# Attention in a stage of its own, and the first FFN products by Strassen's seven products on pairs of batches

## The chip, the cores and the metric

One NeuronCore of a Trainium2 chip runs the whole program. The metric is the device time of one execution in microseconds, the median of three runs for the kernel before. TensorE (PE) multiplies, VectorE (DVE), ScalarE (ACT) and GpSimd (POOL) do the work on tiles, and SyncE (SP) issues most transfers between DRAM and the on-chip memory.

## What is computed

Sigmoid attention for 8 batches, 12 heads, 448 positions and a head width of 64, then a bilinear feed-forward part on the 3584 tokens. All inputs are float32.

```python
scores = scale * np.matmul(q, k.transpose(0, 1, 3, 2)) - np.log(S)
attn = 1.0 / (1.0 + np.exp(-scores))
x = (attn @ v).transpose(0, 2, 1, 3).reshape(B * S, H * D)   # 3584 x 768
a = x @ w1                                                    # 768 x 1024
b = x @ w2
h = a * b @ w3                                                # 1024 x 1024
return h @ w_out                                              # 1024 x 768
```

## The kernel before, in words

Products are made in two ways. A float32 matmul is issued as it is, and shows as two matmul records. An fp32r matmul is one record; to keep precision each operand is split into a rounded part and a rest (`split`, lines 72 to 74), and a product is three fp32r matmuls: high by high, high by low, low by high.

Heads go in 48 pairs (two heads of 64 fill 128 rows). The first 13 pairs (`PLAIN`) use float32: a chunk of 128 positions takes two score matmuls (line 201), one on rows 0 to 63 and one on rows 64 to 127 of the array, and two sums with v (line 253), one on each half of the array's columns. Between the score and the sum stands one sigmoid on ACT (line 184). The weights w1 and w2, which come as 64-bit words, are decoded meanwhile by ACT (line 83) and DVE (lines 90 to 106), and split into fp32r parts that stay on chip.

The other 35 pairs use fp32r on the full array (lines 204, 230 and 260). They take 28 matmuls of 448 columns for a pair, two sigmoids for a chunk (one rounded, one full) and a subtraction on DVE (line 222). Into their matmuls the first products `up` (line 377) are mixed, 12 matmuls at a time: x times w1 and x times w2, on tiles of 512 tokens, 18 matmuls for each of 7 x 8 x 2 results, 2016 in all. The result g = a * b goes to `g_dram`.

After attention the last seventh of the first products runs alone, while w_out is decoded. Then w3 times w_out is made once (line 662, 384 matmuls of 384 columns). The last product, g times that matrix, is made by Strassen's seven products on pairs of batches (`products`, line 695, 1008 matmuls of 448 columns in four blocks); its operands are sums of blocks of g, made on DVE and ACT by `plain_operands`, `sum_operands` and `late_operands` from tiles `graw` that are loaded from `g_dram` into four buffers. Their names are a11, a12, s2, s3, a22, s1, s4 in the order of use.

The order on PE and SP is that of the code (`manual_schedule`), on ACT and POOL too in the attention's first part; the other engines' order is set by a scheduler when the program is built.

## Time and profile before

| | before |
|---|---|
| median of three runs | 1054.52 us (1053.53 to 1056.56) |
| profiled execution, its own time | 1054.23 us |
| its span, first to last instruction | 1052.4 us |
| PE busy | 1040.3 us, 99% |
| DVE busy | 796.3 us, 76% |
| ACT busy | 593.6 us, 56% |
| POOL busy | 163.1 us, 15% |
| moved by DMA | 164.41 MB, 156 GB/s over the span |
| granted TensorE clock, mean | 1.000 of full speed |

The busy time of an engine is the time in which at least one of its instructions runs. Matmuls overlap, so the mean length of one is longer than the distance from one to the next; that distance is read from the start times or from a stretch divided by its count. A wait of an engine is shown with what ended it.

### The profile page before, as it was taken

The page shows a single profiled execution, that of the slowest core. Times are in us where ns is not written, and L with a number is a line of the kernel's source. Part 1 is how long each engine was busy: PE and PEld are TensorE (multiplying, and loading weights), DVE is VectorE, ACT ScalarE, POOL GpSimd, SP SyncE. Part 2 cuts the span into 40 slices and gives each one's busy share as a digit, 9 for nine tenths or more (in the row PEclk, how much of TensorE's full clock was granted, in tenths as well). Part 3 has the DMA queues.
Part 4 walks back from the last instruction along what each step waited for, and adds up shares of the span by engine and source line. Part 5 has one row for each costly group of instructions (what it writes and reads, how often), then busy time and mean ns, then how long its engine had stood idle before and what let it go on. Part 6 is the DMA issues. An engine that isn't in the chain of part 4 may idle for free.

```text
span 1052.4 us, 14185 instructions
## 1 busy us (share of the span) xinstructions
PE 1040.3 (99%) x4820; PEld 847.4 (81%) x4820; DVE 796.3 (76%) x1254; ACT 593.6 (56%) x877; POOL 163.1 (15%) x249
## 2 busy tenths in 40 slices
PE   9999999999999999999999999999999999999998
PEld 3222788888888888888888888878899999999997
DVE  6998788877887778887878877668826677768672
ACT  6887766666666766676676666652324443323230
POOL 0000423323131322323232332100000000000000
PEclk9999999999999999999999999999999999999999
DMA  8676474564546554464455635144324555656542
GB/s 271 218 229 213 129 198 112 150 168 124 151 130 169 147 146 127 135 168 134 133 149 149 169 112 149 48 159 126 116 93 144 184 185 194 218 179 216 182 148 79
DMA packets 117255, 164.41 MB, mean 156 GB/s; under 512 B 9984, under 2 KB 95168, under 8 KB 117184
## 3 DMA queue, kind: packets, MB, share of 16 engines
q1 hardware_dynamic: 117184, 163.52, 51.9%
q8 instruction: 38, 0.62, 0.3%
q14 instruction: 33, 0.27, 0.1%
HBM read 124.16 MB, written 39.32 MB: 155 GB/s over the span
## 4 chain that ended last, share of the span: by engine, by line
PE 89%; DVE 5%; DMA 3%; ACT 1%; issue 1%; SPq 0%; ACTq 0%; DVEq 0%
PE up L377 41%; PE up L695 20%; PE av L260 9%; PE sp L204 8%; PE up L662 5%; PE av L253 2%; PE sp L201 2%; PE sp L230 1%; DMA graw<-g_dram 1%; DVE f L98 1%; DVE raw L103 1%; DMA raw<-w 1%; DMA raw<-w_out 1%; DVE w L74 1%; PE up L427 1%
## 5 line engine op out<-in xcount | busy, mean ns | idle before, releaser
L377 PE MATMUL up<-xh,w 128*128 128x512 f32 x1344 | 438.9, 391 | 1.4 <-DVE g L391 1.4
L377 PEld LDWEIGHTS up<-xh,w 128*128 128x128 f32 x1344 | 252.4, 188 | 54.8 <-ACT f L83 1.8
L377 PE MATMUL up<-xl,w 128*128 128x512 f32 x672 | 263.1, 392 | 0.0
L184 ACT ACTIVATE ah<-sp,bias 128x896 fp32r<-128x896 f32 x105 | 106.1, 1011 | 124.5 <-PE sp L204 124.5
L222 DVE TENSOR_TENSOR al<-sp,ah 128x896 fp32r<-128x896 f32 x105 | 114.4, 1090 | 63.2 <-ACT sp L184 62.4
L377 PEld LDWEIGHTS up<-xl,w 128*128 128x128 f32 x672 | 126.2, 188 | 23.3
L74 POOL TENSOR_TENSOR kl<-kk,kh 128x896 fp32r<-128x896 f32 x35 | 74.7, 2134 | 395.7 <-DVE kh L73 255.4
L695 PE MATMUL up<-gs,w 128*128 128x448 f32 x576 | 119.3, 367 | 0.0
L695 PEld LDWEIGHTS up<-gs,w 128*128 128x128 f32 x576 | 108.1, 188 | 9.9
L184 ACT ACTIVATE sp<-sp,bias 128x896 f32<-128x896 f32 x105 | 102.0, 972 | 0.0
L260 PE MATMUL av<-ah,vs 128*128 128x448 f32 x280 | 92.0, 369 | 0.4 <-DVE t L192 0.4
L695 PE MATMUL up<-ga,w 128*128 128x448 f32 x432 | 89.5, 366 | 0.0
L695 PEld LDWEIGHTS up<-ga,w 128*128 128x128 f32 x432 | 81.1, 188 | 7.1
L204 PE MATMUL sp<-qs,kh 128*128 128x448 f32 x210 | 77.4, 369 | 0.0
L260 PE MATMUL av<-al,vs 128*128 128x448 f32 x210 | 77.4, 368 | 0.0
L204 PE MATMUL sp<-qs,kl 128*128 128x448 f32 x210 | 77.2, 368 | 0.0
L74 POOL TENSOR_TENSOR vs<-vv,vs 128x256 fp32r<-128x256 f32 x70 | 54.9, 786 | 109.2 <-DVE vs L73 109.2
L73 ACT CAST ga<-graw 128x448 fp32r<-128x448 f32 x48 | 25.7, 566 | 68.6 <-DMA graw<-g_dram 68.6
L244 DVE TENSOR_TENSOR ah<-st,ah 64x448 fp32r<-64x448 f32 x70 | 44.2, 632 | 25.2 <-ACT st L184 23.7
L184 ACT ACTIVATE ah<-st,bias 64x448 fp32r<-64x448 f32 x70 | 46.9, 669 | 24.9 <-DVE st L192 23.6
L260 PEld LDWEIGHTS av<-ah,vs 128*128 128x128 f32 x280 | 52.6, 188 | 9.2 <-issue 1.2
L184 ACT ACTIVATE ap<-sp,bias 128x896 f32<-128x896 f32 (+1 forms) x52 | 52.1, 1004 | 13.4 <-PE sp L201 12.5
(77 smaller groups left out, 1504.1 us busy)
## 6 DMA issues: line engine op xcount, KB each, us to landing
graw<-g_dram SPq DMA_DIRECT2D x72, 448.0 KB, 4.4
qq<-qT SPq DMA_DIRECT2D x70, 224.0 KB, 3.7
kk<-kT SPq DMA_DIRECT2D x70, 224.0 KB, 4.4
g_dram<-g SPq DMA_DIRECT2D x56, 256.0 KB, 2.2
raw<-w SPq DMA_DIRECT2D x15, 768.0 KB, 5.4
vv<-vL SPq DMA_DIRECT2D x48, 192.0 KB, 3.8
xr<-x_dram SPq DMA_DIRECT2D x36, 256.0 KB, 4.4
raw<-w3T SPq DMA_DIRECT2D x16, 512.0 KB, 4.3
```

The source lines that it names most:

```text
L73: hi_engine(out=dst_hi, in_=src)
L74: lo_engine.tensor_tensor(out=dst_lo, in0=src, in1=dst_hi, op=ALU.subtract)
L184: nc.scalar.activation(dst, src, AF.Sigmoid, bias=bias[:n], scale=scale)
L201: nc.tensor.matmul(sp[:, j], kh[rows, at:at + n], qs[rows], start=True, stop=True)
L204: nc.tensor.matmul(sp[:, j], k[:, j, at:at + n], qs[:, j], start=m == 0, stop=m == 1)
L222: nc.vector.tensor_tensor(out=al, in0=sp, in1=ah, op=ALU.subtract)
L244: nc.vector.tensor_tensor(out=a[others, j], in0=t[rows], in1=a[rows, j], op=ALU.subtract)
L253: nc.tensor.matmul(accs[0][cols, :S], v[:ops[0].shape[0], c, cols], ops[0][:, j], start=first, stop=last,)
L260: nc.tensor.matmul(accs[j][:, :S], v[:, c, j].rearrange("p u d -> p (u d)"), a[:, j], start=first and m == 0, stop=last and m == len(ops) - 1,
L377: nc.tensor.matmul(acc[:, :TU], w[fc // NH][:, fc % NH, kc], x, start=(kc == 0 and m == 0), stop=(kc == NK - 1 and m == 2),)
L662: nc.tensor.matmul(acc[:, :NM], a[:, jc], w[:, jc, ms], start=(jc == 0 and m == 0), stop=(jc == NF - 1 and m == 2),)
L695: nc.tensor.matmul(acc[:, :TB], w[:, c, ms], g[:, c], start=(c, m) == (0, 0), stop=(c, m) == (NH - 1, 2),)
```

## The change

Attention becomes a stage of its own with nothing mixed in. One pair stays float32. For the other 47, q and k are split on DVE (`qh`, `ql`), and a chunk's scores are six fp32r matmuls, three for each head, with the two heads on rows 0 to 63 and 64 to 127. There is one sigmoid for a chunk, kept in float32, and the sums with v are float32 matmuls on column halves, all eight of a pair in one piece after the next pair's scores. The decoding of w1 and w2 is spread over 44 pairs; DVE also makes four differences of weight blocks (`piece_sum`), which go to `t_dram`.

After attention all first products are made by Strassen's scheme: the two rows of blocks are two batches of x (448 tokens each), the inner dimension is cut in halves of 384, and the columns are w1 and w2. For each of 4 x 8 units there are seven products of nine matmuls of 448 columns, 2016 in all. The block sums of x are made by `operand_x`, the results are put together on DVE by `unit_step`, multiplied on POOL and stored by POOL's own DMA queue. w_out and w3 are decoded meanwhile and stored in DRAM in the same way. The product w3 times w_out keeps its matmuls. The last product keeps its seven products; its operand s2 is now made in the last stage and no longer ahead of it.

```diff
-    PLAIN = 2 * NPAIR + 1
...
+    PLAIN = 1
...
+    def split_pair(p, qk):
+        if p < PLAIN:
+            return (qk,)
+        hi = pa.tile([P, 2, S], F32R, name="qh")
+        lo = pa.tile([P, 2, S], F32R, name="ql")
+        split(hi, lo, qk, nc.vector.tensor_copy, nc.vector)
+        return hi, lo
+
...
+    def scores(qks, c):
         at, n = CHUNKS[c]
-        sp = ps.tile([P, 2, 512], F32, name="sp", bufs=2)[:n, :, :S]
-        for j in range(2):
-            if kl is None:
+        sp = ps.tile([P, 2, 512], F32, name="sp", bufs=3)[:n, :, :S]
+        terms = ((0, 0), (0, 1), (1, 0)) if len(qks) > 1 else ((0, 0),)
+        for m, (kt, qt) in enumerate(terms):
+            for j in range(2):
                 rows = slice(j * D, (j + 1) * D)
-                nc.tensor.matmul(sp[:, j], kh[rows, at:at + n], qs[rows], start=True, stop=True)
-                continue
-            for m, k in enumerate((kh, kl)):
-                nc.tensor.matmul(sp[:, j], k[:, j, at:at + n], qs[:, j], start=m == 0, stop=m == 1)
+                nc.tensor.matmul(
+                    sp[:, j], qks[kt][rows, 1, at:at + n], qks[qt][rows, 0],
+                    start=m == 0, stop=m == len(terms) - 1,
...
+    def attention(sp):
         n = sp.shape[0]
-        if plain:
-            a = pa.tile([P, 2, S], F32, name="ap", tag="ah", bufs=3)[:n]
-            sigmoid(a, sp)
-            return (a,)
-        ah = pa.tile([P, 2, S], F32R, name="ah", tag="ah", bufs=3)
-        sigmoid(ah[:n], sp)
-        sigmoid(sp, sp)
-        if n < P:
-
...
-    def attend(c, ops, v, accs):
-
-        first, last = c == 0, c == NC - 2
...
+    def attend(v, aps):
+        acc = ps.tile([P, 512], F32, name="av", bufs=2)
+        for c, a in enumerate(aps):
             for j in range(2):
                 cols = slice(j * D, (j + 1) * D)
                 nc.tensor.matmul(
-                    accs[0][cols, :S], v[:ops[0].shape[0], c, cols], ops[0][:, j],
-                    start=first, stop=last,
+                    acc[cols, :S], v[:a.shape[0], c, cols], a[:, j], start=c == 0, stop=c == NC - 1
                 )
-            return
-        for j in range(2):
-            for m, a in enumerate(ops):
-                nc.tensor.matmul(
-                    accs[j][:, :S], v[:, c, j].rearrange("p u d -> p (u d)"), a[:, j],
...
+    def piece_sum(fc, kind):
+        f1, f2 = fs[2 * fc], fs[2 * fc + 1]
+        b11, b21, b12, b22 = f1[:, :KH], f1[:, KH:], f2[:, :KH], f2[:, KH:]
+        a, b = {
+            0: lambda: (b12, b11), 3: lambda: (b22, sums[0]), 2: lambda: (b22, b12), 1: lambda: (b21, sums[3])
+        }[kind]()
+        t = sums[kind] = pd.tile([P, KH, P], F32, name="ts", bufs=4)
+        nc.vector.tensor_tensor(out=t, in0=a, in1=b, op=ALU.subtract)
+        hl = pd.tile([P, 2, KH, P], F32R, name="th", bufs=4)
+        split(hl[:, 0], hl[:, 1], t, nc.vector.tensor_copy, nc.vector)
+        store_later(t_dram[fc, kind], hl.bitcast(F32))
+
+    steps = []
+    for i in range(2 * NF):
+        at = 2 + 13 * i // 5
+        steps += [(at - 2, piece_load, (i,)), (at - 1, piece_magnitude, (i,)), (at, piece_decode, (i,))]
+        steps += [(at + 1, piece_split, (i,))]
+        if i % 2:
+            steps += [(at + 1, piece_sum, (i // 2, 0)), (at + 2, piece_sum, (i // 2, 3))]
+            steps += [(at + 2, piece_sum, (i // 2, 2)), (at + 3, piece_sum, (i // 2, 1))]
+    DONE = max(at for at, _, _ in steps) + 1
...
+    def operand_x(name, x1, x2):
+        top, bottom = slice(0, KH), slice(KH, NK)
+        src = {
+            "a11": x1[:, top], "a12": x1[:, bottom], "s3": x2[:, top], "s2": x2[:, top],
+            "a22": x2[:, bottom], "s1": x1[:, top], "s4": x1[:, bottom],
+        }[name]
+        work = {
+            "s3": (x1[:, top], x2[:, top], ALU.subtract),
+            "s2": (x2[:, bottom], x2[:, top], ALU.subtract),
+            "s1": (x2[:, top], x1[:, top], ALU.add),
+            "s4": (x1[:, bottom], x2[:, top], ALU.subtract),
+        }.get(name)
+        if work is not None:
+            nc.vector.tensor_tensor(out=src, in0=work[0], in1=work[1], op=work[2])
+        split(*xop[name], src, nc.scalar.copy, nc.vector)
...
+        now, aps = aps, []
+        if p < len(pairs):
+            qk = parts.pop(p)
+            for c in range(NC):
+                aps.append(attention(scores(qk, c)))
+        if p + 1 < len(pairs):
+            parts[p + 1] = split_pair(p + 1, qks.pop(p + 1))
+        for at, f, args in steps:
+            if at == p and f is not piece_load:
+                f(*args)
+        if DONE <= p < DONE + EARLY:
+            operand_x(names[p - DONE], *xs)
+        if p > 0:
+            b, kc = pairs[p - 1]
+            store_later(x_dram[kc, :, b * S:(b + 1) * S], attend(vvs.pop(p - 1), now))
...
+    def load_sums(fcs, name):
+        for fc in fcs:
+            t = pt.tile([P, 2, KH, P], F32R, name="tw")
+            nc.sync.dma_start(out=t.bitcast(F32), in_=t_dram[fc, KINDS[name]])
+            sets[fc, name] = (t[:, 0], t[:, 1])
...
+    def x_product(fc, name):
+        acc = ps2.tile([P, 512], F32, name="up", tag="acc", bufs=8)
+        ws = weights(fc, name)
+        for c in range(KH):
+            for m, (w, x) in enumerate(((0, 0), (0, 1), (1, 0))):
+                nc.tensor.matmul(
+                    acc[:, :S], ws[w][:, c], xop[name][x][:, c],
+                    start=(c, m) == (0, 0), stop=(c, m) == (KH - 1, 2),
+                )
+        return acc[:, :S]
...
+    def unit_step(g, fc, name):
+        acc = x_product(fc, name)
+        if name == "a11":
+            us[fc] = pu.tile([P, S], F32, name="u")
+            nc.scalar.copy(out=us[fc], in_=acc)
+            return
+        u = us[fc]
+        if name == "a12":
+            rs[fc] = pu.tile([P, 2, S], F32, name="r", bufs=3)
+            add(rs[fc][:, 0], acc, u)
+        elif name == "s3":
+            p7s[fc] = acc
+        elif name == "s2":
+            add(u, acc, u)
+            vs[fc] = pu.tile([P, S], F32, name="v")
+            add(vs[fc], p7s.pop(fc), u)
+        elif name == "a22":
+            add(rs[fc][:, 1], acc, vs[fc])
+        elif name == "s1":
+            add(vs[fc], acc, vs[fc])
+            add(u, acc, u)
+            r = rs[fc]
+            nc.gpsimd.tensor_tensor(out=r[:, 1], in0=r[:, 1], in1=vs.pop(fc), op=ALU.mult)
+        else:
+            add(u, acc, u)
+            r = rs.pop(fc)
+            nc.gpsimd.tensor_tensor(out=r[:, 0], in0=r[:, 0], in1=us.pop(fc), op=ALU.mult)
+            at = 2 * g * S
+            nc.gpsimd.dma_start(
+                out=g_dram[fc, :, at:at + 2 * S].rearrange("p (t s) -> p t s", t=2), in_=r
+            )
...
+            f = decode(raw, magnitude(raw, pu, 2))
+            if i + 2 < len(todo):
+                nxt.append(load_words(todo[i + 2][0], pu, 2))
+            nc.gpsimd.dma_start(out=dst, in_=f)
...
+        for i, name in enumerate(names):
+            for fc in fcs:
+                unit_step(g, fc, name)
+            if nxt is not None and i and names[i - 1] in KINDS:
+                load_sums(nxt[1], names[i - 1])
+            if i in (1, 4) and k:
+                take(decodes, 1)
+            if turn:
+                operand_x(name, *xs)
+            if nxt is None and i < 4:
+                load_out(*list(wo_tags)[2 + i])
+            if nxt is None and i in (4, 5):
+                w3_chunk(i - 4)
+        if k % NH == 1 and g + 1 < NG:
+            xs = load_xs(g + 1)
...
-    early = itertools.chain(plain_operands(0), sum_operands(0, ("s2",)))
+    early = plain_operands(0)
...
-        stage = spare[:, c % 2]
+        w3 = w3s.pop(i)
+        if not second:
+            stage = px2.tile([P, 4, NM], F32, name="stage", tag="s4", bufs=1)
...
+    for name in ("s2", "s1", "s4", "s3", "a22"):
+        operand(p5, name)
+    total = p5.tile([P, NH, TB], F32, name="total", bufs=1)
...
-    prepare_ = itertools.chain(sum_operands(0, ("s3", "a22")), late_operands(0))
+    prepare_ = itertools.chain(
+        sum_operands(0, ("s2",)), sum_operands(0, ("s3", "a22")), late_operands(0)
+    )
```

On PE, in the attention of before, a piece of the order from the fp32r pairs: `sp` are scores, `up` the first products, each row an instruction or several of the same form.

```order
L204 MATMUL sp<-qs,kh 128x448
L204 MATMUL sp<-qs,kl 128x448
L204 MATMUL sp<-qs,kh 128x448
L204 MATMUL sp<-qs,kl 128x448
L377 MATMUL up<-xh,w 128x512
L377 MATMUL up<-xl,w 128x512
L377 MATMUL up<-xh,w 128x512 x2
L377 MATMUL up<-xl,w 128x512
L377 MATMUL up<-xh,w 128x512 x2
L377 MATMUL up<-xl,w 128x512
L377 MATMUL up<-xh,w 128x512 x2
L377 MATMUL up<-xl,w 128x512
```

The same place after the change, one pair p from its second row on: 22 of its 24 score matmuls (`qh`, `ql` are the parts of q and k), then the sums of pair p - 1.

```order
L166 MATMUL sp<-ql,qh 128x448 x2
L166 MATMUL sp<-qh,ql 128x448 x2
L166 MATMUL sp<-qh 128x448 x2
L166 MATMUL sp<-ql,qh 128x448 x2
L166 MATMUL sp<-qh,ql 128x448 x2
L166 MATMUL sp<-qh 128x448 x2
L166 MATMUL sp<-ql,qh 128x448 x2
L166 MATMUL sp<-qh,ql 128x448 x2
L166 MATMUL sp<-qh 64x448 x2
L166 MATMUL sp<-ql,qh 64x448 x2
L166 MATMUL sp<-qh,ql 64x448 x2
L183 MATMUL av<-ap,vv 64x448 x8
```

What moved: the `up` rows have left the attention, the scores went from four full-array matmuls to six half-array ones for a chunk, and the sums with v stand in one piece.

On DVE, before, near the end of the stage of w3 times w_out: `spare<-graw` is the sum that s3 and s1 start from (`total` in the code), `w` are parts of the weight sums.

```order
L574 TENSOR_TENSOR spare<-graw 128x448
L574 TENSOR_TENSOR graw<-graw 128x448
L574 TENSOR_TENSOR spare<-spare 128x384
L574 TENSOR_TENSOR spare<-graw 128x448
L74 TENSOR_TENSOR w<-spare,w 128x384
L574 TENSOR_TENSOR graw<-graw 128x448
L74 TENSOR_TENSOR w<-spare,w 128x384
L574 TENSOR_TENSOR spare<-spare 128x384 x2
L74 TENSOR_TENSOR w<-spare,w 128x384 x3
L574 TENSOR_TENSOR spare<-spare 128x384
```

After the change this is what DVE does at the start of the last stage: `gs_7222` is s2, `o` and `u` take results of the last product from PE.

```order
L74 TENSOR_TENSOR gs_7222<-graw,gs_7222 128x448 x3
L512 TENSOR_TENSOR graw<-graw 128x448
L512 TENSOR_TENSOR o<-up,u 128x448
L512 TENSOR_TENSOR graw<-graw 128x448
L74 TENSOR_TENSOR gs_7222<-graw,gs_7222 128x448
L512 TENSOR_TENSOR o<-up,u 128x448 x2
L512 TENSOR_TENSOR u<-up,u 128x448
L512 TENSOR_TENSOR total<-graw 128x448
L74 TENSOR_TENSOR ga_7226<-graw,ga_7226 128x448
L512 TENSOR_TENSOR graw<-graw 128x448
```

What moved: the first two `total` rows stood inside the stage of w3 times w_out, ahead of its last weight sums; now the first one stands in the last stage, behind the four splits of s2 and a result of the third of the seven products.

## Rows read from the trace of the kernel before

**Rows 1.** The page: busy us by engine (share of the span), instructions.

```profile
PE 1040.3 (99%) x4820; PEld 847.4 (81%) x4820; DVE 796.3 (76%) x1254; ACT 593.6 (56%) x877; POOL 163.1 (15%) x249
```

**Rows 2.** The chain that ended last, shares by engine and line.

```profile
PE up L377 41%; PE up L695 20%; PE av L260 9%; PE sp L204 8%; PE up L662 5%; PE av L253 2%; PE sp L201 2%; PE sp L230 1%; DMA graw<-g_dram 1%; DVE f L98 1%; DVE raw L103 1%; DMA raw<-w 1%; DMA raw<-w_out 1%; DVE w L74 1%; PE up L427 1%
```

**Rows 3.** Windows: stretch, busy us (instructions) by engine, clock, DMA share, GB/s.

```profile
7.60:107.20 99.60, 95.28 (x413) 24.35 (x412) 92.17 (x134) 81.52 (x102) 2.60 (x4) 1.00 0.75 234
107.20:708.90 601.70, 599.89 (x2714) 508.20 (x2712) 471.89 (x685) 400.97 (x565) 160.27 (x242) 1.00 0.50 141
709.00:774.50 65.50, 65.50 (x289) 54.24 (x290) 45.88 (x102) 17.22 (x34) 0.00 (x0) 1.00 0.35 105
774.40:842.50 68.10, 66.99 (x385) 66.34 (x384) 40.10 (x68) 30.00 (x57) 0.00 (x0) 1.00 0.46 159
842.50:1052.40 209.90, 206.48 (x1010) 189.12 (x1008) 145.13 (x263) 61.88 (x117) 0.00 (x0) 1.00 0.54 176
```

**Rows 4.** Timeline of PE, fp32r attention: start, length, line, tiles.

```profile
302.31 0.37 PE L204 MATMUL sp<-qs,kh 128*128 128x448 f32 x1
...
302.93 0.37 PE L204 MATMUL sp<-qs,kl 128*128 128x448 f32 x1
```

**Rows 5.** Timeline of PE, float32 pairs; x2 rows are a chunk's second records.

```profile
59.48 0.97 PE L253 MATMUL av<-ap,vv 128*64 128x448 f32 x4
59.90 0.55 PE L253 MATMUL av<-ap,vv 128*64 128x448 f32 x2
60.38 1.02 PE L201 MATMUL sp<-qp 64*128 64x448 f32 x4
60.86 0.54 PE L201 MATMUL sp<-qp 64*128 64x448 f32 x2
61.33 0.97 PE L253 MATMUL av<-ap,vv 128*64 128x448 f32 x4
62.23 0.97 PE L201 MATMUL sp<-qp 64*64 64x448 f32 x4
```

**Rows 6.** Timeline of PE's weight loads, float32 pairs.

```profile
60.38 0.30 PEld L201 LDWEIGHTS sp<-qp 64*128 64x128 f32 x4 [0.70 <-issue]
```

**Rows 7.** Groups of instructions: busy us, mean ns | idle before, releaser.

```profile
L184 ACT ACTIVATE ap<-sp,bias 128x896 f32<-128x896 f32 (+1 forms) x52 | 52.1, 1004 | 13.4 <-PE sp L201 12.5
L278 ACT COPY t<-av 128x448 f32<-128x448 f32 x7 | 3.7, 530 | 0.0
L83 ACT ACTIVATE f<-raw 128x768 f32<-128x768 f32 x15 | 13.9, 925 | 0.6 <-DMA raw<-w 0.6
L73 ACT CAST w<-f 128x768 fp32r<-128x768 f32 x16 | 13.2, 824 | 4.4 <-DVE f L106 4.4
L73 DVE CAST kh<-kk 128x896 fp32r<-128x896 f32 x35 | 21.9, 625 | 1.1 <-DMA kk<-kT 0.5
L222 DVE TENSOR_TENSOR al<-sp,ah 128x896 fp32r<-128x896 f32 x105 | 114.4, 1090 | 63.2 <-ACT sp L184 62.4
L106 DVE TENSOR_TENSOR f<-f,raw 128x768 f32<-128x768 f32 x15 | 14.4, 958 | 0.5
L102 DVE TENSOR_SCALAR raw<-f 128x768 uint32<-128x768 uint32 x15 | 8.4, 563 | 0.5
L74 DVE TENSOR_TENSOR w<-spare,w 128x384 fp32r<-128x384 f32 x28 | 14.8, 554 | 7.6 <-ACT w L73 7.5
L574 DVE TENSOR_TENSOR u<-up,u 128x448 f32<-128x448 f32 x36 | 22.2, 618 | 6.2 <-PE up L695 6.2
```

**Rows 8.** Waits of PE in the float32 pairs (8 to 107 us): us, times, longest.

```profile
PE av L253 <- ACT ap L184: 3.5, 5, 1.4
```

**Rows 9.** Timeline of DVE, start of the last stage: tiles of `total` and s3.

```profile
851.32 0.63 DVE L574 TENSOR_TENSOR spare<-graw 128x448 f32<-128x448 f32 x1 [1.44 <-DMA graw<-g_dram]
...
855.11 0.62 DVE L574 TENSOR_TENSOR spare<-graw 128x448 f32<-128x448 f32 x1 [0.49 <-DMA graw<-g_dram]
...
857.79 0.62 DVE L74 TENSOR_TENSOR gs<-graw,gs 128x448 fp32r<-128x448 f32 x1
```

More of the change, by code (lines that the diff above doesn't have):

```diff
@@ L120, in sigmoid_attention_bilinear_ffn, with take @@
-    bias = pm.tile([P, 1], F32, name="bias", bufs=1)
+    def take(stream, n):
+        for _ in range(n):
+            next(stream, None)
+    ET = mybir.EngineType
+    later_pools = ExitStack()
+    praw = later_pools.enter_context(tc.tile_pool(name="praw", bufs=1, side="right"))
+    phase_d = ExitStack()
+    pd = phase_d.enter_context(tc.tile_pool(name="pd", bufs=2, side="right"))
+    phase_a = ExitStack()
+    pa = phase_a.enter_context(tc.tile_pool(name="pa", bufs=2, side="left"))
+    ps = phase_a.enter_context(tc.tile_pool(name="ps", bufs=3, space=PSUM))
@@ L144, in load_v @@
-    def load_v(b, hp):
-        vv = pa.tile([P, NC, 2 * D], F32, name="vv")
+        qk = pa.tile([P, 2, S], F32, name="qk", bufs=4)
+        for i, src in enumerate((qT, kT)):
+            nc.sync.dma_start(out=qk[:, i], in_=src[b, heads].rearrange("h d s -> (h d) s"))
+        return qk
+    def load_v(p):
+        b, hp = pairs[p]
+        vv = pa.tile([P, NC, 2 * D], F32, name="vv", bufs=4)
         cols = slice(hp * 2 * D, (hp + 1) * 2 * D)
@@ L396, in take, with store_later, flush, piece_load @@
-    def take(stream, n):
-        for _ in range(n):
-            next(stream, None)
-    ET = mybir.EngineType
+    later = []
+    def store_later(dst, src):
+        later.append((dst, src))
+    def flush():
+        while later:
+            dst, src = later.pop(0)
+            nc.sync.dma_start(out=dst, in_=src)
+    pieces = [words(w, slice(fc * P, (fc + 1) * P)) for fc in range(NF) for w in (w1, w2)]
+    raws, fs = {}, {}
+    def piece_load(i):
+        raws[i] = load_words(pieces[i], pd, 2)
@@ new lines, in piece_magnitude, with piece_decode, piece_split @@
+    def piece_magnitude(i):
+        fs[i] = magnitude(raws[i], pd, 4)
+    def piece_decode(i):
+        decode(raws.pop(i), fs[i])
+    def piece_split(i):
+        fc, second = divmod(i, 2)
+        if second:
+            split(w2h[:, fc], w2l[:, fc], fs[i][:, KH:], nc.scalar.copy, nc.vector)
+        else:
+            half, at = divmod(fc, NH)
+            split(w1h[half][:, at], w1l[half][:, at], fs[i], nc.scalar.copy, nc.vector)
+    sums = {}
+    def piece_sum(fc, kind):
[9 more added lines that the diff above has]
+        store_later(t_dram[fc, kind], hl.bitcast(F32))
@@ new lines, in sigmoid_attention_bilinear_ffn @@
+    parts = {0: split_pair(0, qks.pop(0))}
+    xs = None
+    names = ("a11", "a12", "s3", "s2", "a22", "s1", "s4")
+    aps = []
+    EARLY = 3
+    for p in range(len(pairs) + 1):
+        flush()
+        for step in steps:
+            if step[0] == p and step[1] is piece_load:
+                step[1](*step[2])
+        if p + 3 < len(pairs):
+            qks[p + 3] = load_pair(p + 3)
+        if p + 2 < len(pairs):
+            vvs[p + 2] = load_v(p + 2)
+        if p == DONE:
+            phase_d.close()
+            px1 = later_pools.enter_context(tc.tile_pool(name="px1", bufs=1, side="right"))
+            for name in names[:EARLY]:
+                new_x(px1, name)
+        if p == 2 * NPAIR + 4:
+            xs = load_xs(0)
+        now, aps = aps, []
[13 more added lines that the diff above has]
+            store_later(x_dram[kc, :, b * S:(b + 1) * S], attend(vvs.pop(p - 1), now))
```

477 lines of the change are left out of this document (131 added, 346 removed).

## The prediction

> **What bounds the kernel now.** First the busy shares: PE runs 99% of the span, the next engine, DVE, 76% [rows 1]. Then the chain that ended last: it is PE almost throughout, 41% in the first products (line 377), 20% in the last product (line 695) [rows 2]. So what counts is how long each stage of PE work is, and whether another engine becomes the limit where the change thins out PE's work. The windows cut the span into stages [rows 3]: 7.6 us of start, 99.6 us for the 13 float32 pairs, 601.7 us for the 35 fp32r pairs with six sevenths of the first products mixed in, 65.5 us for the last seventh, 68.1 us for w3 times w_out, 209.9 us for the last product with its tail. They add up to 1052.4 us. The profiled execution took 1054.23 us, 1.8 more than its span, and the median of the runs is 0.3 above it.
>
> From these stages come the prices of matmuls, as distances from one to the next. In the fp32r attention three steps take 302.93 - 302.31 = 0.62 us, 0.207 us a step for 448 columns [rows 4]. In the last product 1008 matmuls of 448 columns take 206.4 us (PE's busy time less the two from the stage before), 0.2048 each; in the last seventh of the first products 288 of 512 columns take 65.5 us, 0.2274 each [rows 3]. In the long stage the 35 x 28 = 980 attention matmuls at 0.207 are 202.9 us, so the 1728 first products take 398 us of the 601.7, 0.230 each. Before, then, attention costs 99.6 + 202.9 = 302.5 us of PE and the first products 398 + 65.5 = 463.5 us.
>
> **First products.** Strassen's scheme has 4 x 8 x 7 x 9 = 2016 matmuls, as many as before; each has 448 columns and not 512. The price of the same form of matmul with 448 columns is that of the last product: 2016 x 0.2048 = 412.8 us. That removes 50.7 us. Bounds: 0.2067 a step as in the attention gives 416.7, and a column share of 448/512 of the 0.2274 gives 0.199 and 401 us; I take the measured form.
>
> **Scores.** A chunk has three steps, if the two heads' matmuls, on different row halves, run side by side. The float32 pairs price this mode [rows 5]. The second records of a chunk's sums begin 59.90 - 59.48 = 0.42 us after the first, those of its scores 60.86 - 60.38 = 0.48. The sums load 64 columns of weights, the scores 128; so some 0.05 to 0.06 us go to each 64 columns of a load that nothing hides, 0.107 for 128, and the other 0.373 is what two rounds of 448 columns take at 2.4 GHz, the level of the granted clock of 1.00 [rows 3]. The whole chunk takes 61.33 - 60.38 = 0.95 us; four records in turn would take 4 x 0.373 = 1.5, so the two heads do run side by side, and their weight loads too, four in 0.30 us [rows 6]. The change to column halves adds 0.95 - 0.48 - 0.373 = 0.10. For fp32r on row halves no row has a price. At 0.207 a step, with one load of 0.107 and two changes of shape (the last chunk has 64 columns of weights), a pair's scores take 12 x 0.207 + 0.31 = 2.8 us. Bounds: 0.187 a step (448 columns at 2.4 GHz) gives 2.55; both heads one after the other give 24 x 0.207 + 0.31 = 5.3.
>
> **Sums with v.** A chunk's sums took 62.23 - 61.33 = 0.90 us with a change of shape at both ends [rows 5]. In one piece of four chunks the changes are fewer: eight records of 0.373 and two entries of about 0.15 (0.10 and 0.05) are 3.3; I take 3.4 and keep 3.6 as the upper bound.
>
> **A pair** is then 6.2 us (5.8 to 6.4 while the halves run side by side), 47 pairs 291.4, and the one float32 pair 4 x (0.95 + 0.90) = 7.4: 298.8 us against 302.5 before. Attention gains next to nothing; the seven products carry the change.
>
> **What has to hide behind 6.2 us a pair.** ACT: four sigmoids at 1.004 and a copy of 0.53 are 4.55 us; 16 pieces over 44 pairs add 0.925 for the magnitude and 0.82 or half of it for the rounding, 0.56 a pair: 5.1 [rows 7]. DVE: the split of q and k 0.625 + 1.09 = 1.7; a piece's decoding has three operations near 0.96 and three near 0.56, 4.6 us, its low part 0.95 or 0.55, and each two pieces need four weight sums of 0.55 + 0.35 + 0.55: 16.5 us for two pieces, which is 3.2 a pair: 4.9 [rows 7]. In the float32 pairs DVE ran 92.17 and ACT 81.52 of 99.6 us [rows 3], and PE still waited only 3.5 us for a sigmoid [rows 8]. Here both have a fifth of the time free, and PE has a whole pair of scores between a sigmoid and the sums that use it. I allow 4 us. Queued behind ACT's wait for the sums (its copy of `av`) are the next pair's sigmoids; but those can't start before the first chunk's scores are done, 0.7 us later, and the copy takes 0.53. DMA moves, by the tiles' sizes, 896 KB of q, k, v and x for a pair and 24.6 MB of weights and weight sums over 44 pairs, about 1.5 MB in 6.2 us, 240 GB/s; the float32 pairs ran at 234 [rows 3]. On SP a pair's stores, which wait for the copy `t` and for DVE's sums, stand ahead of the loads; the loads are for two and three pairs later, 12 us, so a store that waits 1 or 2 us delays nothing.
>
> **What has to hide behind the first products.** A group of two units is 126 matmuls, 25.8 us. DVE has 14 results of 0.618, 8.7 us [rows 7], and two decoded pieces of w_out or w3, some 7 us: 16 of 25.8. At the three turns to new batches it makes seven operands of 1344 columns, 11 operations of three times 0.618, 20.4 us, and 29 in all: over by 3, while eight PSUM banks hold 8 x 9 x 0.2048 = 14.7 us of products. Hidden, if nothing else is late; I allow 4 us for the start of the stage (new operands and the first weight sums from DRAM) and the turns. The two products on POOL and its stores wait for nothing that PE needs within a group.
>
> **The last two stages.** w3 times w_out keeps its matmuls, 68.1 us; its single `stage` has 8.3 us of PE time for about 6 us of DVE work, and PSUM banks behind that. In the last stage s2's fourth block is loaded first, and s3's four blocks come behind it. Before, two blocks of `total` were made 855.11 - 851.32 = 3.8 us apart and the last s3 part was done at 858.4 [rows 9], 6.5 us before its product. After, five blocks follow at that pace: the last `total` near 866.5 on that clock and s3 at 869.6, while its matmul would come at 866.6. So 3 us lost, once.
>
> **Sum.** 7.6 + 7.4 + 291.4 + 412.8 + 68.1 + 209.9 = 997.2; with 4 + 4 + 3 of waits 1008.2 us of span, plus 1.8 outside it: **1010 us**, 4.2% below the 1054.23 of the profiled execution. What a measurement of this kernel can tell from no change is 0.3%, about 3 us.
>
> **Rivals.** (1) Weight loads stand bare on row halves. What each step needs is a load of 0.107 ahead of 0.187 of columns, in the same rows that are multiplying: 12 x 0.294 + 0.2 = 3.7 and 3.6 for the sums, 7.3 us a pair, 52 us more: 1062, slower than before. It decides from 0.08 us of bare load a step on. For it: a load is bare on every entry in [rows 5]. Against it: the second records' loads lie within 0.30 us of the first's start [rows 6], while the first still multiply in the same rows until 0.48, and the second follow with no gap. The Trainium skill, "TensorE: Matmul & The Clock Gate", section "The mechanism", says that a weight load overlaps running matmuls only when its row group differs. By that rule this rival holds; the trace disagrees with it inside a float32 matmul, and no row shows two matmuls in sequence on one row half. Chance 0.10.
>
> (2) fp32r halves don't run side by side at all: 5.3 + 3.6 = 8.9 us a pair, 127 us more, 1137. Against it is only that float32 halves do. Chance 0.07.
>
> (3) Attention is set by ACT and DVE in each other's way. In the float32 pairs a pair took 99.6 / 13 = 7.66 us, with the same sigmoids and DVE at 92% [rows 3]. If half of that difference to 6.2 stays, a pair is 6.9 and the time 1043. Chance 0.10.
>
> (4) DVE or the transfers fall behind in the first products: three turns at 8 us and a late start give 25 us more, 1035. The seven products' gain is then halved. Chance 0.08.
>
> **Chances.** The forecast 0.62, its own range 985 to 1034 (5.8 to 6.6 us a pair, 4 to 15 of waits); a better time than that 0.03. Cases 3 and 4 stay faster than before; of case 1 some 0.03 falls within 0.3% of before. So faster 0.83, same 0.03, slower 0.14. The range with the forecast, 3 and 4 is 985 to 1048.
>
> **What would show it.** Right: distances of 0.2 us between score steps with the two heads' matmuls at almost the same time, a pair every 6.2 us, DVE and ACT near 80% there; 0.205 us a matmul in the first products; a wait of PE for s3 early in the last stage. Wrong: score matmuls evenly 0.2 us apart (2), pairs near 7.3 us with no wait of PE on another engine (1), or with waits on sigmoids or `ql` (3); waits of PE on PSUM at the turns (4).

## The result, and the profile after

The changed kernel took **996.09 us** (median of four runs, 994.95 to 997.99) against 1054.2 for the kernel before beside it: ratio 0.9447, 95% interval 0.9426 to 0.9468. The forecast was 1010, 14 us too high, with 996 in its range. The same kernel, run again beside the experiments, took 1008.61 us (1007.89 to 1008.92), ratio 0.957 (0.9552 to 0.9587), while the kernel before stayed at 1053.8. Those 12 us between two sets of runs of one program come from the first products and are followed up below; they matter for every comparison here.

The page of the profiled execution after (span 996.2 us), busy time by engine, answers to [rows 1]: PE keeps its 99%, the others fall.

```profile
PE 981.8 (99%) x5336; PEld 781.4 (78%) x5336; DVE 713.6 (72%) x1078; ACT 402.4 (40%) x544; POOL 116.1 (12%) x128
```

Windows of the profile after: attention, the first products, then four stretches at the start of the last stage (columns as in [rows 3]; the third number from the end is the granted clock).

```profile
13.50:302.20 288.70, 287.44 (x1874) 136.96 (x1872) 205.78 (x304) 227.88 (x270) 0.00 (x0) 1.00 0.73 238
302.20:705.70 403.50, 403.42 (x2017) 378.59 (x2018) 315.88 (x437) 73.60 (x94) 112.41 (x120) 1.00 0.73 246
...
787.20:794.60 7.40, 7.40 (x37) 6.58 (x36) 4.59 (x9) 2.27 (x4) 0.00 (x0) 1.00 0.98 322
794.60:802.00 7.40, 3.00 (x8) 1.36 (x7) 5.80 (x11) 2.83 (x5) 0.00 (x0) 0.73 0.78 241
802.00:809.40 7.40, 4.48 (x12) 3.21 (x11) 6.55 (x12) 2.65 (x5) 0.00 (x0) 0.50 0.72 211
809.40:816.80 7.40, 7.40 (x33) 6.68 (x32) 5.92 (x12) 3.28 (x7) 0.00 (x0) 0.84 0.68 196
```

PE is busy throughout attention and the first products; DVE is busy 71% and ACT 79% of attention. The loss lies in 14.8 us at the start of the last stage: PE works 3.00 and 4.48 of 7.40 us, and the granted clock falls from 1.00 (2.4 GHz) to 0.50 (1.2 GHz). The waits of PE after, us in total, times, longest, show nothing else of note (left out is one of 1.4 us at the very start):

```profile
PE up L632 <- ACT gs L73: 6.5, 3, 2.7
...
PE up L632 <- DVE gs L74: 0.8, 2, 0.5
PE sp L166 <- ACT ap L175: 0.7, 1, 0.7
PE up L366 <- ACT t L187: 0.6, 1, 0.6
```

PE's timeline in attention (start, length, tiles) answers to [rows 4, 5]. The two heads' records of a score step (x2) stand together, a step every 0.20 us after the first one's 0.31. The scores take 154.60 - 151.81 = 2.79 us, the sums 151.81 - 148.50 = 3.31, a pair 6.10.

```profile
148.50 3.38 PE L183 MATMUL av<-ap,vv 128*64 128x448 f32 x16
151.81 0.47 PE L166 MATMUL sp<-qh 64*128 64x448 f32 x2
152.12 0.36 PE L166 MATMUL sp<-ql,qh 64*128 64x448 f32 x2
152.31 0.37 PE L166 MATMUL sp<-qh,ql 64*128 64x448 f32 x2
...
154.60 1.72 PE L183 MATMUL av<-ap,vv 128*64 128x448 f32 x8
```

Stage by stage, from the first matmul of one to the first of the next, in us: the forecast with its waits, the profiled execution after, and the one of the repetition (1006.9 us of span).

| stage | forecast | after | repeated |
|---|---|---|---|
| start, to the first score | 7.6 | 7.0 | 7.4 |
| attention | 298.8 + 4 | 295.2 | 294.2 |
| first products | 412.8 + 4 | 403.3 | 416.7 |
| w3 times w_out | 68.1 | 66.6 | 66.6 |
| last stage | 209.9 + 3 | 224.0 | 222.1 |

### The profile page after: what moved, and what is told of

It reads as the page before. It is cut to its first block, busy times and chain, and to the rows that moved or that the text cites. A ratio compares the mean times of both kernels' runs of the same rounds, so it can differ in the third digit from the quotient of the medians.

```text
span 996.2 us, 14461 instructions
## 1 busy us (share of the span) xinstructions
PE 981.8 (99%) x5336; PEld 781.4 (78%) x5336; DVE 713.6 (72%) x1078; ACT 402.4 (40%) x544; POOL 116.1 (12%) x128
## 4 chain that ended last, share of the span: by engine, by line
PE 94%; DMA 3%; DVE 2%; ACT 1%; issue 0%; SPq 0%; DVEq 0%; ACTq 0%
PE up L366 41%; PE up L632 19%; PE av L183 15%; PE sp L166 13%; PE up L596 7%; DMA graw<-g_dram 1%; DMA x_dram<-t 1%; DMA raw<-w 1%; PE sp L290 1%; DVE gs L74 0%; DVE graw L512 0%; DVE w L74 0%; DVE total L512 0%; DVE ga L74 0%; DVE u L512 0%
## 5 line engine op out<-in xcount | busy, mean ns | idle before, releaser
L175 ACT ACTIVATE ap<-sp,bias 128x896 f32<-128x896 f32 x192 | 182.5, 1005 | 25.2 <-PE sp L166 20.3
L366 PE MATMUL up<-xs,tw 128*128 128x448 f32 x864 | 178.0, 362 | 0.0
L366 PEld LDWEIGHTS up<-xs,tw 128*128 128x128 f32 x864 | 162.2, 188 | 10.6
L183 PE MATMUL av<-ap,vv 128*64 128x448 f32 (+1 forms) x768 | 161.9, 551 | 0.0
L366 PE MATMUL up<-xa,w 128*128 128x448 f32 x576 | 117.9, 362 | 0.6 <-ACT t L187 0.6
L366 PEld LDWEIGHTS up<-xa,w 128*128 128x128 f32 x576 | 108.0, 188 | 8.5 <-ACT t L187 1.4
L166 PE MATMUL sp<-qh 64*128 64x448 f32 (+1 forms) x376 | 77.0, 403 | 0.7 <-ACT ap L175 0.7
L166 PE MATMUL sp<-qh,ql 64*128 64x448 f32 (+1 forms) x376 | 70.0, 363 | 0.0
L166 PE MATMUL sp<-ql,qh 64*128 64x448 f32 (+1 forms) x376 | 69.4, 361 | 0.0
L596 PE MATMUL up<-wo,w 128*128 128x384 f32 x384 | 66.7, 334 | 0.0
L596 PEld LDWEIGHTS up<-wo,w 128*128 128x128 f32 x384 | 66.6, 188 | 0.0
## 6 DMA issues: line engine op xcount, KB each, us to landing
qk<-qT SPq DMA_DIRECT2D x48, 224.0 KB, 4.2
qk<-kT SPq DMA_DIRECT2D x48, 224.0 KB, 4.4
x_dram<-t SPq DMA_DIRECT2D x48, 224.0 KB, 2.3
```

What stands on the lines that cost most here:

```text
L166: nc.tensor.matmul(sp[:, j], qks[kt][rows, 1, at:at + n], qks[qt][rows, 0], start=m == 0, stop=m == len(terms) - 1,)
L175: nc.scalar.activation(a, sp, AF.Sigmoid, bias=bias[:n], scale=scale)
L183: nc.tensor.matmul(acc[cols, :S], v[:a.shape[0], c, cols], a[:, j], start=c == 0, stop=c == NC - 1)
L366: nc.tensor.matmul(acc[:, :S], ws[w][:, c], xop[name][x][:, c], start=(c, m) == (0, 0), stop=(c, m) == (KH - 1, 2),)
L596: nc.tensor.matmul(acc[:, :NM], w3[a][:, jc], wo[w][:, jc % JG], start=(jc == 0 and m == 0), stop=(jc == NF - 1 and m == 2),)
```

## The experiments

The twelve runs in one table: median, length of the first products and the distance from one of their matmuls to the next, length of the last stage (from its first matmul; the expectations count from the end of the stage before, which makes it 0.2 us less), PE's waits in it, and for how long the clock stood at 1.2 GHz there. All but the median are read from the one profiled execution of each run. For e8 the time is that of the profiled execution. e7's four executions lie between 1026.02 and 1040.44 us, so that its stage says more than its median. Before, the last stage took 209.9 us [rows 3].

| run | median | first products | distance | last stage | waits | 1.2 GHz |
|---|---|---|---|---|---|---|
| changed kernel | 996.09 | 403.3 | 0.2000 | 224.0 | 7.3 | 13.7 |
| e1 loads ahead | 1004.59 | 416.7 | 0.2067 | 218.8 | 3.4 | 6.8 |
| e2 stores on POOL | 1005.25 | 416.7 | 0.2067 | 218.5 | 4.7 | 6.8 |
| e3 one pass | 1004.35 | 416.7 | 0.2067 | 217.9 | 3.5 | 6.8 |
| e4 weight layout | 1009.09 | 416.7 | 0.2067 | 222.4 | 6.3 | 10.2 |
| e5 repeated | 1008.61 | 416.7 | 0.2067 | 222.1 | 6.5 | 10.2 |
| e6 terms in sequence | 1009.84 | 416.7 | 0.2067 | 223.0 | 6.3 | 10.2 |
| e7 plain scores | 1036.89 | 418.3 | 0.2067 | 222.1 | 6.3 | 10.2 |
| e8 a11 twice | 1054.64 | 460.9 | 0.2000 | 223.1 | 7.0 | 10.2 |
| e9 disturbed | 1008.48 | 416.7 | both | 222.1 | 6.7 | 10.2 |
| e10 filler on a11 | 1006.01 | 403.3 | 0.2000 | 234.5 | 16.1 | 17.1 |
| e11 filler on s2, 70 columns | 999.20 | 411.7 | both | 216.4 | 1.4 | none |
| e12 all kept | 1000.01 | 416.9 | 0.2067 | 213.1 | 0.5 | none |

**The last stage.** PE's timeline and SP's DMA issues of the kernel after, side by side, show s3 late and why; DVE's timeline has the first and the last of the four blocks of `total`, from which s3 is made.

```profile
786.77 8.29 PE L632 MATMUL up<-gs,w 128*128 128x448 f32 x39
796.59 0.48 PE L632 MATMUL up<-gs,w 128*128 128x448 f32 x1 [1.52 <-ACT gs L73]
...
800.69 1.78 PE L632 MATMUL up<-gs,w 128*128 128x448 f32 x3 [2.35 <-ACT gs L73]
805.12 0.74 PE L632 MATMUL up<-gs,w 128*128 128x448 f32 x1 [2.66 <-ACT gs L73]
```

```profile
762.93 16.09 SPq L519 DMA_DIRECT2D graw<-g_dram  x5
783.37 2.66 SPq L638 DMA_DIRECT2D out<-o  x2
786.13 1.82 SPq L519 DMA_DIRECT2D graw<-g_dram  x4
788.00 0.70 SPq L638 DMA_DIRECT2D out<-o  x1
792.23 5.66 SPq L519 DMA_DIRECT2D graw<-g_dram  x4
```

```profile
791.04 0.62 DVE L512 TENSOR_TENSOR total<-graw 128x448 f32<-128x448 f32 x1 [0.97 <-DMA graw<-g_dram]
...
802.71 0.62 DVE L512 TENSOR_TENSOR total<-graw 128x448 f32<-128x448 f32 x1 [1.42 <-DMA graw<-g_dram]
```

The stores of `o` (line 638) stand ahead of the last eight loads of `graw` in SP's queue and wait for their results. Is it the queue, or the bytes? Four runs ask this. e1:

```diff
-                take(prepare_, 1)
+                take(prepare_, 2 if n == 0 and i == 0 else 1)
```

> In the first block of the last stage the preparing steps are taken two at a time during the first product, so that SP issues all but one chunk of the loads for s3 ahead of the first stores of o. Queue theory (the loads for s3 come late because they stand in SP's queue behind stores that wait for o): TensorE's waits on s3 after 787 us fall from about 15 us to under 4, the granted clock stays at 2.4 GHz there, the last stage takes 211 to 215 us in place of 223.8, and the whole 984 to 988. Transfer theory (the bytes decide, the stage moves 293 to 322 GB/s with the DMA engines 0.90 to 0.98 busy while s3 is loaded): the loads start earlier but share the same engines; the last stage stays at 220 us or more, the whole 993 to 998.

e2, in `store`:

```diff
-        nc.sync.dma_start(out=outT[mc * P:(mc + 1) * P, t * TB:(t + 1) * TB], in_=o)
+        (nc.gpsimd if t < 2 else nc.sync).dma_start(out=outT[mc * P:(mc + 1) * P, t * TB:(t + 1) * TB], in_=o)
```

> The stores of the first block of the last stage go out through POOL's queue and the loads for s3 stay where they were in SP's order, with no store ahead of them that waits. Queue theory: the same gain as with the loads put ahead, 984 to 989 us, the loads for s3 issued as soon as their buffers come free, about 8 us earlier than in the changed kernel. Transfer theory: no gain, 993 to 998.

e3, with e1's edit:

```diff
-        sum_operands(0, ("s2",)), sum_operands(0, ("s3", "a22")), late_operands(0)
+        sum_operands(0, ("s2", "s3", "a22")), late_operands(0)
```

> The first block of the last stage makes s2, s3 and a22 in one pass over the rows, as the later blocks do, so that 8 loads of 0.46 MB fall away and total is made once; two steps are taken at a time during the first product. Queue theory: nothing beyond what the loads put ahead give, 984 to 989 us, or a little worse, since the last chunk of s2 now stands behind work for s3. Transfer theory: this is the run that gains, 984 to 989, and the one with only the loads put ahead is not (993 or more).

e4:

```diff
-        w = (pw if i < 6 else p4).tile([P, 2, NH, NM], F32R, name="w")
+        w = (pw if i < 6 else p4).tile([P, 2, NMC, NH, P], F32R, name="w")
```

> The weights of the last stage are laid out in memory with the chunks of one output tile side by side, as they lie in the first products; nothing else changes. Layout theory (the weights' layout is why matmuls of the same shape stand 0.200 us apart in the first products and 0.203 to 0.206 in the last stage): the last stage's steps fall to 0.200, 1008 of them give 3 to 5 us, 991 to 994 us in all. Rival (the layout has no part in it): 0.203 to 0.206 stay, 995 to 998.

The medians of all four lie above 996, and none of these edits touches the first products, which took 13.4 us more in each; the last stage has to be compared by itself, with the repetition's 222.1 (where nothing in it was edited it took 222.1 to 224.0). e1 and e2 shorten it alike, by 3.3 and 3.6 us, and e3, which saves 8 loads, by 4.1. So SP's order was a cause, and fewer bytes add less than a microsecond (in e3 the last parts of s2 also come later). The blocks of `total` show it too. Counted from the stage's first matmul, the first one begins after 18.9 us in the kernel after and in the repetition, and after 13.1 in e1 and 13.7 in e2; the last one after 30.5 and 29.1, and after 25.4 and 26.6. In e2 the last of these loads is issued 3.4 us earlier than in the kernel after, not the 8 that were expected.

The queue theory's 211 to 215 us was not reached either: half of the waits stayed (3.4 us in e1), with the clock at 1.2 GHz for 6.8 us. What is left is put down to s2: made during w3 times w_out before, and in the last stage's first two products after, ahead of s3's work on DVE and the same loads. No run makes it early again, so this part is argued and not shown. e4's layout changed nothing.

**The clock after the wait.** e10 has, with e1's edit, before the first product with s3:

```diff
+            if n == 0 and i == 3:
+                extra = ps2.tile([P, 512], F32, name="up", tag="acc", bufs=8)
+                for _ in range(20):
+                    nc.tensor.matmul(extra[:, :TB], wop["b11"][0][:, 0, :P],
+                                     gop["a11"][0][:, 0], start=True, stop=True)
```

> As the run with the loads put ahead, and before the first product with s3 TensorE runs 20 added matmuls on operands that it has (their result is not used), about 4.1 us, in the place of the 3.4 us that it waited there. Theory (half of what is left of the loss is the clock: it fell to 1.2 GHz for 6.8 us after the wait, which costs 3.4 us): with no wait the clock stays at 2.4 GHz through the first block, and the last stage takes 215 to 216.5 us in place of 218.65 although it has more matmuls. Rival (the clock falls anyway, or DVE and the transfers are as late after the filler): 218.5 to 222.5 us.

The run does not answer its question. By then a11 is being written for the next block, and the added matmuls waited for it; PE's timeline of e10:

```profile
809.57 6.84 PE L664 MATMUL up<-ga,w 128*128 128x448 f32 x20 [16.06 <-ACT ga L73]
```

e11 uses s2 and t2 with 18 matmuls, and in the first products e9's added matmul, always of 70 columns.

> Two edits in different stages, on top of the loads put ahead. First products: each of the 16 groups begins with one added matmul of 70 columns whose result is overwritten, the length after which a group went from 0.2067 to 0.2000 in the run before. Theory that the length of what breaks the run sets the spacing that is caught next: every group, or every one that follows a group at the same spacing, comes out alike, all at 0.2000 if 70 columns do it always (the stage 404 to 406 us, the whole 988 to 993). Rival, that it falls by chance, or by finer timing than a column: a mixture again, most groups at 0.2067 (14 of 16 were), the stage 412 to 418. Last stage: 18 added matmuls, this time on s2 and t2, which stay in place, before the first product with s3. Theory (the wait of 3.4 us made the clock fall to 1.2 GHz for 6.8 us): no wait, no fall, 215 to 216.5 us in place of 218.65. Rival (the clock falls anyway, or s3 is as late after the filler): 218.5 to 222.5.

For the last stage the theory held: 216.4 us, though 3.7 us of matmuls were added. Windows around s3, of e1 and then of e11, the last line of each is 4.8 us without a wait; the clock is the third number from the end:

```profile
807.60:815.00 7.40, 3.98 (x13) 2.34 (x12) 6.77 (x14) 2.59 (x5) 0.00 (x0) 0.85 0.92 303
815.00:822.40 7.40, 7.40 (x27) 6.64 (x26) 6.88 (x13) 2.64 (x6) 0.00 (x0) 0.69 0.69 212
...
814.60:819.40 4.80, 4.80 (x14) 4.28 (x13) 4.40 (x9) 1.63 (x3) 0.00 (x0) 0.50 0.58 163
```

```profile
802.50:810.00 7.50, 6.20 (x29) 5.06 (x27) 5.39 (x12) 2.27 (x4) 0.00 (x0) 1.00 0.79 255
810.00:817.40 7.40, 7.28 (x36) 6.84 (x37) 7.02 (x14) 1.95 (x4) 0.00 (x0) 1.00 0.72 226
...
820.00:824.80 4.80, 4.80 (x25) 4.50 (x25) 4.39 (x9) 1.91 (x4) 0.00 (x0) 1.00 0.42 142
```

In e1 PE is fully busy from 815.0 on and still does 27 matmuls in 7.4 us; in e11, with no fall, 36. By the start times the matmuls at 1.2 GHz stand 0.373 us apart, which is 448 columns at 1.2 GHz and nothing more, where they stand 0.207 apart at 2.4. There are 13 such steps in e1: the slow clock costs 13 x 0.166 = 2.2 us, and a little more in steps that hold a wait as well. The expectations' 3.4 us, half of the 6.8, was too high, since PE also waited in that time, and 0.373 is less than twice 0.207. Matmul by matmul, e11 falls 3.7 us behind e1 with its 18 added ones, gains 5.4 over the next 27, where e1 waits and then runs at 1.2 GHz, and 0.8 more over the next 117, nearly all 0.2000 apart in place of 0.2067: 2.4 us shorter in all. e12, which has the same 18 and not the matmuls of 70 columns in each group, shows no fall either. e7 shows the clock at another place: ahead of its first products TensorE waits 1.6 us where the other runs wait 0.6, the clock then stands at 1.2 GHz for 3.4 us, and the stage takes 418.3 us for 416.7.

**Attention.** e6 tests whether the two heads have to take turns for their halves to run side by side:

```diff
-        for m, (kt, qt) in enumerate(terms):
-            for j in range(2):
-                rows = slice(j * D, (j + 1) * D)
+        for j in range(2):
+            rows = slice(j * D, (j + 1) * D)
+            for m, (kt, qt) in enumerate(terms):
```

> In the fp32r scores the three terms of one head follow each other, then those of the other head, in place of the heads taking turns; the work is the same. Theory (the scores cost 2.81 us a pair because each step's two halves run beside each other, the next weights loading meanwhile, which needs neighbours on different row halves): of 24 matmuls only those at a change of head still run side by side, 16 to 20 steps of 0.20 us, 3.4 to 4.9 us a pair, and up to 7 with the loads bare at 0.31; attention 30 to 100 us longer than 289 us, and up to 190. Rival (the order within a tile has no part in it): 2.8 us, attention within 3 us of 289.

The theory fell. From the first sums to the last, 288.8 us against 287.1 in e5. PE's timeline of e6 shows the steps as before, both heads' records together, although the code issues three terms of one head and then three of the other; the records don't name the head, but each head has one matmul of each form in a chunk, so the second head's first matmul starts 10 ns after the first head's, and 0.30 us ahead of the first head's second one, which stands before it in the code.

```profile
151.33 0.48 PE L166 MATMUL sp<-qh 64*128 64x448 f32 x2
151.64 0.37 PE L166 MATMUL sp<-ql,qh 64*128 64x448 f32 x2
151.84 0.37 PE L166 MATMUL sp<-qh,ql 64*128 64x448 f32 x2
```

e7 undoes the fp32r scores (`PLAIN = 48`):

> All 48 pairs score in float32, as pair 0 does, so the splitting of q and k on VectorE falls away and the score tiles take 16 matmuls a pair in place of 24. Theory (TensorE bounds attention, a plain pair's scores take 3.35 us and an fp32r pair's 2.81): 47 pairs times 0.54 = 25 us more, attention 312 to 316 us. Rival (ScalarE or VectorE set the pace of a pair, or what a pair gains is lost in waits): no change or less than 10 us, since VectorE loses about 2.5 us of work a pair.

Attention by the same measure takes 314.4 us, 27.4 more than e5, 0.58 a pair: TensorE sets its pace, as the theory said. Windows of attention, e7 and then e5:

```profile
13.70:328.10 314.40, 313.34 (x1506) 104.66 (x1504) 133.48 (x215) 228.15 (x270) 0.00 (x0) 1.00 0.68 218
```

```profile
13.90:300.90 287.00, 287.00 (x1874) 136.53 (x1872) 205.33 (x304) 227.01 (x269) 0.00 (x0) 1.00 0.74 239
```

**The first products.** e8 repeats one product of the seven:

```diff
+        for _ in range(2 if name == "a11" else 1):
             for c in range(KH):
```

> In the first products the product a11 is computed twice into the same accumulators (the second pass starts them anew): 288 matmuls more with no vector work, transfer or wait added. Theory (the stage is bound by TensorE alone, so that what Strassen's seven in place of eight saved is its matmuls' own time): 288 times 0.2000 to 0.2067, 57.6 to 59.5 us more in the stage. Rival (VectorE, the transfers of the sums or the turns set its pace and TensorE has slack): under 45 us more.

The stage took 460.9 us with matmuls at 0.2000, against 403.3: 57.6 more, which is 288 x 0.2000. Nothing but TensorE bounds it. The run's other execution took 1070.68 us and left no trace, so what made it longer stays open.

e5 is the changed kernel without an edit.

> The changed kernel with no edit, beside the runs below. In the four runs so far the matmuls of the first products stood 0.2067 us apart, in the changed kernel's own profile 0.2000, though no instruction of that stage or ahead of it was altered: 13.4 us over 2016 matmuls. Theory that the place decides (the chip, or where the program and its data lie in that load): here too 0.2067 and 1007 to 1011 us. Rival, that the edits of the last stage did it in some indirect way: 0.2000 and 995 to 998 us.

It came out at 0.2067 in all of the stage, so the edits of the last stage are not the reason. The chip alone isn't either: e8 ran on the same one as e1 to e7, at 0.2000. Windows of the same 40 us in the kernel after and in e5: 202 records against 195, at the same clock and with less traffic in the slower one.

```profile
320.00:360.00 40.00, 40.00 (x202) 37.54 (x201) 28.87 (x44) 3.30 (x6) 15.09 (x16) 1.00 0.80 268
```

```profile
320.00:360.00 40.00, 40.00 (x195) 36.38 (x195) 28.96 (x44) 2.94 (x5) 14.49 (x15) 1.00 0.77 250
```

e9 breaks the run of equal matmuls at each of 16 groups, in `x_product` ahead of the first of 126 matmuls (`odd` is 64 in the first group, 66 in the second, up to 94):

```diff
+        if odd:
+            nc.tensor.matmul(acc[:, :odd], ws[0][:, 0], xop[name][0][:, 0, :odd], start=True, stop=True)
```

> In the first products each group of two column chunks (126 matmuls) begins with one added matmul whose result is overwritten, of 64 columns in the first group and 2 more in each that follows, up to 94 in the sixteenth; nothing else changes. So far the matmuls of one execution stood either all 0.2000 or all 0.2067 us apart in this stage. Theory that the spacing is caught at the stage's start and held until something breaks the run of equal matmuls: the groups of one execution now differ, some at 0.2000 and some at 0.2067, and the stage takes between 404 and 418 us. Rival, that it is fixed for the execution (by the load or the chip): all sixteen groups have the same spacing, 0.2000 or 0.2067.

The theory held: within one execution groups 1 and 4 (64 and 70 columns) ran at 0.2000, the other fourteen at 0.2067. Windows inside the first four groups of e9, then of e11 with its 70 columns in every group:

```profile
302.00:326.00 24.00, 24.00 (x122) 22.52 (x121) 19.40 (x26) 7.16 (x8) 2.06 (x2) 1.00 0.92 315
328.00:352.00 24.00, 24.00 (x118) 21.84 (x117) 15.53 (x24) 2.31 (x4) 6.75 (x8) 1.00 0.70 219
354.00:378.00 24.00, 24.00 (x118) 21.83 (x117) 14.70 (x23) 2.42 (x4) 6.41 (x7) 1.00 0.93 322
380.00:404.00 24.00, 24.00 (x122) 22.52 (x121) 23.83 (x30) 8.71 (x9) 7.40 (x9) 1.00 0.69 224
```

```profile
303.00:327.00 24.00, 24.00 (x122) 22.52 (x121) 19.64 (x26) 7.17 (x8) 2.23 (x3) 1.00 0.91 322
329.00:353.00 24.00, 24.00 (x118) 21.84 (x117) 14.35 (x24) 2.19 (x4) 6.45 (x7) 1.00 0.66 217
355.00:379.00 24.00, 24.00 (x122) 22.52 (x121) 16.07 (x26) 2.40 (x4) 6.80 (x8) 1.00 0.97 331
380.00:404.00 24.00, 24.00 (x118) 21.84 (x117) 23.83 (x30) 8.69 (x9) 7.50 (x8) 1.00 0.67 209
```

In e11 all 16 groups alternate, 0.2000, 0.2067, 0.2000: 70 columns take the one spacing to the other, both ways. So it is not chance, and of the theory its second form holds: every group that follows one at the same spacing comes out alike. e12 keeps e1's edit and the filler, one matmul of 70 columns at the start of the stage, and one in each later block of the last stage:

```diff
+                if n and (i, mc) == (2, 1):
+                    nc.tensor.matmul(acc[:, :70], wop[wb][0][:, 0, :P], gop[ga][0][:, 0, :70],
+                                     start=True, stop=True)
```

> The loads put ahead and the 18 added matmuls before s3, as in the run before; of the added matmuls of 70 columns only the one at the start of the first products stays, and one each stands in the last stage's blocks 1 to 3 after the first third of the product with s2, where all runs so far went on at 0.2067. Theory (70 columns take TensorE from a spacing of 0.2067 to 0.2000, and the spacing is then held while nothing breaks the run and the operands lie alike): the first products all at 0.2000, 403.5 to 404 us; the last stage 1 us a block less, 212.5 to 214 us in place of 216.2; the whole 986 to 990. Rival (what the entry catches varies, and the last stage's spacing hangs on where the operands lie, whatever stands ahead): 0.2067 in the first products, 417 us, 0.2067 in blocks 1 to 3, 216 us, the whole 1001 to 1004; or one of the two, 990 to 1001.

One of the two. In the last stage each of blocks 1 to 3 went from 0.2067 to 0.2000 at that point and stayed so until the next block's a11: 213.1 us, 3.3 less than in e11. At the start of the first products the same matmul caught 0.2067 this time. Windows of e12:

```profile
320.00:360.00 40.00, 40.00 (x195) 36.40 (x194) 29.31 (x44) 2.83 (x5) 13.90 (x15) 1.00 0.79 258
857.00:891.00 34.00, 34.00 (x171) 31.86 (x171) 22.12 (x40) 8.68 (x17) 0.00 (x0) 1.00 0.61 198
```

e12 beats the changed kernel at equal spacing (1000.01 us against 1008.61), but not the first runs' 996.09; no run has both its last stage and 0.2000 in the first products, which by estimate would be 13.4 us less than its profiled execution's 999.98, near 987.

## Why the prediction was right, and where it was off

- **Attention** was priced nearly right. Scores were 2.79 us a pair (2.8), sums 3.31 (3.4), a pair 6.10 (6.2): 47 x 0.1 = 4.7 us too much. The allowance of 4 us for waits was not needed (0.7). The first step of a pair, 0.31 us, is 0.11 longer than the others, as its one bare load of 0.107 says. That attention itself gains little holds: 295.2 us against 302.5, an estimate from the mixed stage of before.
- **Rival 1**, bare weight loads on row halves: refuted by steps 0.20 us apart, and not 0.294; the next step's load into the same rows costs nothing visible. The Trainium skill, on which the rival leaned ("TensorE: Matmul & The Clock Gate", section "The mechanism"), says that a load overlaps running matmuls only when its row group differs; the trace disagrees, with its 0.20 us a step on the same rows. **Rival 2**, halves one after the other: refuted by the same rows, and e6 shows that even the order of issue hardly matters (288.8 us against 287.1). **Rival 3**, ACT and DVE as the pace: e7 refutes it.
- **First products.** That the seven products carry the change is shown, and that they are TensorE's alone (e8; no wait but 0.6 us, so **rival 4** falls). The step that was off in size is "the price of the same form of matmul with 448 columns is that of the last product": 0.2048 was a mean over stretches of the last product before at 0.2027, 0.2053 and 0.2067 us, and another stage needn't stand at that mean. In the first runs it was 0.2000, 9.5 us less, close to the 0.199 that the prediction worked out as its lower bound and set aside; in the repetition 0.2067, 4 us more. The 4 us for waits were not needed.
- **w3 times w_out**: 66.6 for 68.1, carried over with a wait that is gone.
- **Last stage**: "So 3 us lost, once" is the step that was off most: the stage is 14.1 us longer in the profile after. The pace of `total` that it took from [rows 9], 3.8 us a block, was right (791.04 to 802.71 for three: 3.9). What it had wrong is when the first one begins: by its sum 12.5 us into the stage, measured 18.9, because SP's stores of `o` now stand ahead of the loads. With that order changed it is 13.1 (e1), the stage is 3.3 to 3.6 us shorter (e1, e2), and the waits that stay, 3.4 us, are near the 3 that were forecast. It also left out that PE's wait brings the clock down (e11: the fall is gone with the wait). By start times, 12.4 of the 14.1 us lie in the steps of s3 that wait or run at 1.2 GHz, 2.2 of them in 13 matmuls 0.373 us apart; the rest is, in equal parts, the distance of the later matmuls and a longer tail.

Against the profiled execution after, the errors are -7.6 for attention with its waits, -13.5 for the first products, -1.5, -0.6 and +11.1, in all -12; they partly cancelled. In the repetition they are -8.6, -0.1, -1.5, -0.2 and +9.2: that its 1008.61 us lies so near to 1010 is luck, attention taken too long against a last stage taken too short.

## What to carry to other kernels

Before an edit is credited with one or two per cent, compare the distance between equal matmuls in a stage that it doesn't touch: here 13 us hung on it alone. Where a change moves preparing work into another stage, read the order of DMA issues on SP in that stage, because a store that waited for a result held the loads behind it (3.3 to 3.6 us here). A wait of a few microseconds on TensorE was paid twice here, in the wait and in the clock; the matmuls that filled it cost 3.7 us and saved 5.4.

## What was not expected of the hardware

- Equal fp32r matmuls (448 columns, 128 x 128) have at least two steady distances at a granted clock of 1.00: 0.2000 and 0.2067 us, 480 and 496 cycles at 2.4 GHz. Each lasts for hundreds of matmuls, over changes of weights, with a DMA share of 0.66 to 0.97, and can change when the run is broken (e9, e11, e12). For a single matmul by itself the Trainium skill ("TensorE: Matmul & The Clock Gate", section "Back-to-back issue gap") gives columns / 2.4 + 2.5 ns, an estimate of 189 ns for 448 columns; no run here shows a steady distance that short for fp32r at this clock.
- In the last stage the distance also changes from product to product with no gap: 0.2027 with a11 and a12, 0.2067 from s2 on, in every block of e1, e4 and e5 that no wait disturbed. The 0.2027 is a mean: the distances repeat in fives between 0.199 and 0.207 us. So the place of the operands may have a part in it, but not the whole: e4 lays the weights out otherwise and keeps both distances, and e12 takes the same products from 0.2067 to 0.2000 with one matmul of 70 columns. What sets the distance, and what the start of a stage catches, stays open.
- At 1.2 GHz the same matmuls stand 0.373 us apart (13 steps of e1), 448 cycles, where at 2.4 GHz the steady distances are 480 and 496 cycles: what is added at the fast clock is gone at the slow one.
- On two row halves of the array a matmul can start ahead of one that was issued before it (e6: 0.30 us). The Trainium skill ("TensorE: Matmul & The Clock Gate", section "The mechanism") has matmuls start and end strictly in the order of the program; the trace of e6 disagrees for the starts.
